# Longest-first order of the attention value products, two-queue load of the first block of x, and a replanned start, in a fused LayerNorm, window-attention and MLP kernel

## The chip, the cores and the metric

The kernel runs on one core of one Trainium2 chip. Times are microseconds (us) of device time for one execution. A profile's span is the part of it that the engines' records cover, here about 2 us less. A profile shows one execution.

Engine names: PE is TensorE's matmul, PEld its weight load, DVE is VectorE, ACT ScalarE, POOL GpSimd, SP SyncE.

## The reference

S = 2048 tokens, D = 512, bfloat16 in and out. A is causal attention over a window of 256 tokens, with 32 heads of 16; B is a gated MLP without an activation, with F = 1792.

```python
xn  = layernorm(x)                                   # no weights, eps 1e-5
qkv = (xn @ wqkv)                                    # 32 heads x 16
p   = softmax(where(0 <= i - j < 256, q @ k.T / 4, -1e9))
A   = (p @ v).reshape(S, D) @ wo
B   = ((xn @ w_gate) * (xn @ w_up)) @ w_down
out = x + A + B
```

## The kernel before

The kernel has a small planner: a list scheduler, run when the kernel is built, which emits the instructions of all engines in the order in which its own cost numbers say that they become ready. So a changed cost number changes the order of the program.

Work goes by chunks of 512 tokens (T = 0..3) and four groups of heads (c), which gives 16 **value blocks**. Keys and queries are in blocks of 64. A **segment** (k, q, m, at) says that key block k meets m query blocks from q on, and lies at block `at` of a strip P of exponentiated scores. Its m, times 64, is the number of columns of its matmuls.

```python
def layout(T):
    if T == 0:
        return [[(2, 2, 4, 0), (4, 4, 4, 4)], [(0, 0, 5, 0), (5, 5, 3, 5)],
                [(1, 1, 5, 0), (6, 6, 2, 5), (7, 7, 1, 7)], [(3, 3, 5, 0), (2, 6, 1, 5)]]
    return [[(3, 3, 5, 0), (-3, 0, 2, 5), (-4, 0, 1, 7)], [(2, 2, 5, 0), (6, 6, 2, 5), (7, 7, 1, 7)],
            [(0, 0, 5, 0), (5, 5, 3, 5)], [(1, 1, 5, 0), (-2, 0, 3, 5)], [(-1, 0, 4, 0), (4, 4, 4, 4)]]

def i_values(self, T, c, strips, banks):
    segments = [(P, s) for P, batch in strips for s in batch]
    for n, (P, (k, q, m, at)) in enumerate(segments):
        U, j = divmod(8 * T + k, 8)
        for lane in range(2):
            rows = slice(64 * lane, 64 * lane + 64)
            for e in range(4):
                self.nc.tensor.matmul(
                    banks[lane][32 * e:32 * e + 17, 64 * q:64 * (q + m)],
                    lhsT=self.V[U % 3][rows, j, 4 * c + e, 0:17],
                    rhs=P[rows, e, 64 * at:64 * (at + m)],
                    start=n == 0, stop=n == len(segments) - 1, tile_position=(64 * lane, 32 * e), ...)
```

One segment is a **round** of eight small matmuls, one on each 64 x 32 tile of the array, each with its own weight load just before it. I call load and matmul a **pair**. The first four blocks (T = 0) have 9 rounds, with lengths 4,4,5,3,5,2,1,5,1 in units of 64 columns (72 pairs). The other twelve have 12 rounds, 5,2,1,5,2,1,5,3,5,3,4,4 (96 pairs). All of a block's segments add into the same two banks, so their order is free.

The start, the weights of the planner and the loads:

```python
PACE = 2.95                       # the planner's distance between score batches, us
load(nc.sync, self.x[:, 0, :], xv[:, 0, :])
load(nc.scalar, self.x[:, 1, :], xv[:, 1, :])
for n, lo in enumerate((1024, 512, 0)):              # value, key, query weights
    load(nc.sync, self.Wqkv[:, :, lo:lo + 512], w["qkv"][:, :, lo:lo + 512])
    if n:
        load(nc.sync, self.x[:, n + 1, :], xv[:, n + 1, :])
# ... Wg, Wu, the rest of x, Wd in five pieces, Wo
o = self.pe(at, 1.25 if T else 0.87, f"V{v}")        # do_values: what the planner takes a value block to cost
land = (3.75, 3.9, 7.9, 9.6)                         # first_chunk: when blocks 0..3 of x are taken to land
wv, wk, wq = 6.1, 7.3, 9.1                           # and the three parts of Wqkv
```

In the first chunk the planner emits for each block of 128 tokens a *turn* (four transposing matmuls), values, keys and queries.

The softmax here doesn't subtract the row's maximum and nothing guards it: scores larger than these inputs give would overflow.

## Time and profile before

| | before |
|---|---|
| time, median of 3 runs | 267.49 us (267.42 to 268.14) |
| span of the profiled run | 266.0 us |
| PE busy | 97% of the span |
| value blocks: first matmul to the next dense one | 0.95 to 0.97 us (first four), 1.35 us (ten of the other twelve; 1.32 and 1.27 in the two at 203 and 247 us) |
| first gate matmul (the end of the start) | 18.06 us |

These lines are from the page of the kernel before. The first ones are the span and each engine's busy time, then the granted clock in 40 slices (9 is 90% or more) and the shares of the chain of work that ended last, by engine.

```profile
span 266.0 us, 7966 instructions
PE 257.9 (97%) x3423; PEld 131.4 (49%) x3458; DVE 192.8 (72%) x369; ACT 163.0 (61%) x118; POOL 119.8 (45%) x272
PEclk9999999999999999999999999999999999999999
PE 93%; DMA 3%; issue 1%; SPq 1%; DVE 1%
```

PE bounds the kernel. Only PE work that takes less time, an earlier start or a shorter tail can help. The waits view of PE (line: us in total, times, longest) names the few waits there are. All but the slivers called "issue" lie in the first 10 us:

```profile
PE M L203 <- issue: 1.3, 8, 0.2
PE M L193 <- PEq L790: 0.8, 1, 0.8
PE M L602 <- DVE xn L263: 0.4, 1, 0.4
PE M L663 <- ACT xnT L197: 0.3, 1, 0.3
PE M L203 <- DMA Wqkv<-in_A_wqkv_dram: 0.3, 1, 0.3
```

The timeline of PE at the start (start us, duration us, line, shape, count, and in brackets the idle time before it and what ended it), and one line of VectorE's: the first statistics, which start when block 0 of x has landed.

```profile
5.72 0.40 PE L602 MATMUL M<-ident,xn 128*128 128x128 bf16 x4 [0.41 <-DVE xn L263]
6.80 1.06 PE L663 MATMUL M<-Wqkv,xnT 128*64 128x256 bf16 x16 [0.34 <-ACT xnT L197]
9.38 2.85 PE L203 MATMUL M<-xnT,Wqkv 128*128 128x128 bf16 x48 [0.29 <-DMA Wqkv<-in_A_wqkv_dram]
12.07 0.39 PE L602 MATMUL M<-ident,xn 128*128 128x128 bf16 x4
18.06 1.03 PE L203 MATMUL M<-xnT,Wg 128*128 128x512 bf16 x3
3.78 0.69 DVE L576 BATCH_NORM_STATS2 st<-x 128x6 f32<-128x512 bf16 x1 [1.84 <-DMA x<-in_A_x_dram]
```

Turn 0 is at 5.72, the queries at 9.38 wait 0.29 us for their weights, turn 2 is at 12.07, and from the first gate matmul at 18.06 on PE hardly waits.

Two value blocks in the timeline of PE, one of 72 and one of 96 matmuls. The length of a block is the distance from its start to the start of the dense matmul on the next line.

```profile
35.42 1.04 PE L235 MATMUL M<-P,V 64*17 64x256 bf16 x72
36.39 0.39 PE L203 MATMUL M<-xnT,Wg 128*128 128x512 bf16 x1
...
100.30 1.42 PE L235 MATMUL M<-P,V 64*17 64x320 bf16 x96
101.65 1.04 PE L203 MATMUL M<-xnT,Wg 128*128 128x512 bf16 x3
```

The second block again in the windows view of the value line: stretch, then PE's and PEld's busy us with the number of instructions that run in the stretch (one can count in two), granted clock, DMA share, GB/s.

```profile
100.30:100.63 0.33, 0.33 (x32) 0.31 (x33) 1.00 0.07 25
100.63:100.95 0.32, 0.32 (x48) 0.31 (x29) 1.00 0.22 80
100.95:101.30 0.35, 0.35 (x40) 0.35 (x38) 1.00 0.90 290
101.30:101.65 0.35, 0.35 (x32) 0.13 (x14) 1.00 0.05 12
```

### The profile page before, as it was taken

To read this page: it belongs to the slowest core of one execution; us is meant where nothing else is said; L and a number is where in the kernel's file an instruction comes from. 1 tells how busy PE (TensorE), PEld (TensorE's weight loads), DVE (VectorE), ACT (ScalarE), POOL (GpSimd) and SP (SyncE) were. 2 spreads that over 40 slices of the span, in tenths; PEclk is the share of its full clock that TensorE was granted. 3 is DMA by queue.
4 is the path that set the end of the run, shared out by engine and by line. 5 is a ranking of instruction groups with operands and counts; after the bars stand their busy time and mean duration, and the time that the engine had idled before them with its cause. 6 is when DMAs were issued, how large, how long until landed. Compare 5 with 4: busy or idle time off the path is not lost.

```text
span 266.0 us, 7966 instructions
## 1 busy us (share of the span) xinstructions
PE 257.9 (97%) x3423; PEld 131.4 (49%) x3458; DVE 192.8 (72%) x369; ACT 163.0 (61%) x118; POOL 119.8 (45%) x272
## 2 busy tenths in 40 slices
PE   7999999999999999999999999999999999999995
PEld 7884444554445444465445354446544454444562
DVE  4889887888997628696997539787784439697504
ACT  3637676667667657678676566667876666656000
POOL 1403665654356361808265552708173543618000
PEclk9999999999999999999999999999999999999999
DMA  7999920000000400000002310000000000000002
GB/s 218 377 373 349 189 43 0 4 2 0 4 2 20 101 20 26 0 2 2 2 0 43 81 39 2 2 4 0 2 2 22 20 22 23 0 2 0 2 2 80
DMA packets 17251, 13.88 MB, mean 52 GB/s; under 512 B 7104, under 2 KB 17216, under 8 KB 17216
## 3 DMA queue, kind: packets, MB, share of 16 engines
q1 hardware_dynamic: 16928, 13.18, 16.9%
q8 instruction: 27, 0.44, 0.8%
q10 hardware_dynamic: 288, 0.20, 0.3%
q14 instruction: 8, 0.07, 0.1%
HBM read 9.70 MB, written 2.10 MB: 44 GB/s over the span
## 4 chain that ended last, share of the span: by engine, by line
PE 93%; DMA 3%; issue 1%; SPq 1%; DVE 1%
PE M L203 70%; PE S L211 9%; PE M L235 7%; PE M L663 5%; DMA Wqkv<-in_A_wqkv_dram 2%; SPq L148 1%; DMA out_dram<-xn 1%; PE S L203 1%; DVE xn L756 1%; PE M L602 0%
## 5 line engine op out<-in xcount | busy, mean ns | idle before, releaser
L487 ACT ACTIVATE P<-S 128x2048 bf16<-128x2048 f32 x76 | 140.9, 1853 | 61.0 <-PE S L211 54.2
L220 POOL TENSOR_SCALAR_AFFINE_SELECT P<-P 64x256 bf16<-64x256 bf16 (+1 forms) x248 | 112.8, 456 | 119.1 <-ACT P L487 106.3
L203 PE MATMUL M<-xnT,Wg 128*128 128x512 bf16 x216 | 57.1, 380 | 0.4
L203 PE MATMUL M<-xnT,Wu 128*128 128x512 bf16 x214 | 56.8, 380 | 0.5
L203 PE MATMUL M<-Wd,hT 128*128 128x512 bf16 (+1 forms) x215 | 50.4, 373 | 1.0 <-issue 0.8
L714 DVE TENSOR_TENSOR hT<-M,gsb 128x512 bf16<-128x512 f32 x56 | 38.0, 678 | 6.0 <-PE M L203 5.7
L199 DVE CAST gsb<-M 128x512 bf16<-128x512 f32 x43 | 29.4, 684 | 5.8 <-PE M L203 5.7
L203 PEld LDWEIGHTS <-hT 128*128 128x128 bf16 x238 | 21.6, 98 | 24.1 <-issue 3.1
L203 PEld LDWEIGHTS <-Wu 128*128 128x128 bf16 x224 | 20.5, 98 | 25.6 <-issue 2.9
L203 PEld LDWEIGHTS <-Wg 128*128 128x128 bf16 x224 | 20.0, 98 | 24.6 <-issue 3.3
L203 PE MATMUL M<-xnT,Wqkv 128*128 128x128 bf16 (+1 forms) x219 | 30.3, 286 | 0.7 <-DMA Wqkv<-in_A_wqkv_dram 0.3
L211 PE MATMUL S<-Q,K 32*128 32x320 bf16 (+3 forms) x720 | 30.1, 254 | 0.3
L523 DVE STREAM_TRANSPOSE at<-M 128x512 f32<-128x512 f32 x32 | 22.3, 707 | 9.2 <-PE M L235 9.1
L211 PEld LDWEIGHTS <-K 32*128 32x128 bf16 x720 | 11.9, 92 | 32.2 <-issue 31.3
L226 DVE TENSOR_TENSOR P<-P,masks 128x512 int16<-128x512 int16 x56 | 22.8, 412 | 6.4 <-ACT P L487 6.3
L274 DVE TENSOR_SCALAR K<-M,own 128x512 bf16<-128x512 f32 x28 | 20.1, 743 | 4.3 <-PE M L203 3.6
L756 DVE TENSOR_TENSOR y<-M,x 128x512 bf16<-128x512 f32 x12 | 8.2, 685 | 20.1 <-PE M L203 20.1
L203 PEld LDWEIGHTS <-Wqkv 128*128 128x128 bf16 x224 | 15.8, 98 | 11.5 <-issue 1.9
L235 PE MATMUL M<-P,V 64*17 64x320 bf16 (+4 forms) x1440 | 21.0, 252 | 0.0
L235 PEld LDWEIGHTS <-V 64*17 64x17 bf16 x1440 | 16.7, 85 | 2.3 <-issue 0.8
L663 PE MATMUL M<-Wqkv,xnT 128*64 128x256 bf16 x256 | 15.7, 274 | 0.3 <-ACT xnT L197 0.3
L203 PE MATMUL M<-Wo,OT 128*128 128x512 bf16 (+1 forms) x61 | 15.0, 372 | 0.4 <-issue 0.3
(51 smaller groups left out, 134.1 us busy)
## 6 DMA issues: line engine op xcount, KB each, us to landing
Wg<-in_B_w_gate_dram SPq DMA_DIRECT2D x2, 896.0 KB, 10.2
Wu<-in_B_w_up_dram SPq DMA_DIRECT2D x2, 896.0 KB, 12.2
Wqkv<-in_A_wqkv_dram SPq DMA_DIRECT2D x3, 512.0 KB, 5.7
Wd<-in_B_w_down_dram SPq DMA_DIRECT2D x4, 384.0 KB, 9.6
out_dram<-y SPq DMA_DIRECT2D x12, 128.0 KB, 1.7
x<-in_A_x_dram SPq DMA_DIRECT2D x1, 1024.0 KB, 14.2
x<-in_A_x_dram SPq DMA_DIRECT2D x1, 512.0 KB, 11.5
Wo<-in_A_wo_dram SPq DMA_DIRECT2D x1, 512.0 KB, 8.0
```

Of the source, the lines that this page charges most:

```text
L199: self.nc.vector.tensor_copy(out=out, in_=in_)
L203: self.nc.tensor.matmul(ps, lhsT=a, rhs=b, start=first and n == 0, stop=last and n == len(pairs) - 1)
L211: self.nc.tensor.matmul(self.S[:, e, 64 * at:64 * (at + m)], lhsT=self.K[U % 3][rows, c, j].rearrange("p l t -> p (l t)"), rhs=self.Q[T % ...
L220: self.nc.gpsimd.affine_select(out=v, in_=v, pattern=[[0, 4], [0, n], [sign, 64]], base=0, fill=0.0, compare_op=ALU.is_gt if kind else ALU ...
L226: self.nc.vector.tensor_tensor(out=v, in0=v, in1=m, op=ALU.bitwise_and)
L235: self.nc.tensor.matmul(banks[lane][32 * e:32 * e + 17, 64 * q:64 * (q + m)], lhsT=self.V[U % 3][rows, j, 4 * c + e, 0:17], rhs=P[rows, e, ...
L274: self.nc.vector.tensor_scalar(out=out, in0=in_, scalar1=own, scalar2=None, op0=ALU.mult)
L487: ex = self.op(f"exp{g}", {"A": (took + 0.06, took + 0.18)}, [o], lambda e: self.nc.scalar.activation(out=P[:, :, 0:hi], in_=self.S[:, :, ...
L523: t = self.op(f"tr{v}", {"V": (0.63, 0.71)}, [o] + ts, lambda e, par=par: nc.vector.transpose(out=self.at[:, :, par, :], in_=self.M[banks[ ...
L663: self.nc.tensor.matmul(self.M[i][64 * lane:64 * lane + 64, 256 * jj:256 * jj + 256], lhsT=self.xnT[T % 2][:, k, tok], rhs=w[:, lane], sta ...
L714: x = self.op(f"u{T}.{f}", {"V": PSUM_COPY["V"]}, [o, ("gate", T, f)], lambda e: self.nc.vector.tensor_tensor(out=self.hT[T % 2][:, f, :], ...
L756: self.nc.vector.tensor_tensor(out=keep["y"][:, cols], in0=self.M[i][:, cols], in1=self.x[:, t, cols], op=ALU.add)
```

## The change

The intent: put the long value products first so that the short ones come with their weights already loaded; get block 0 of x earlier by loading its halves on two queues; and tell the planner of the shorter value blocks and of the landing times, so that it emits the keys of blocks 0 and 1 ahead of their queries.

```diff
-    PACE = 2.95
+    PACE = 2.9
-        load(nc.sync, self.x[:, 0, :], xv[:, 0, :])
+        load(nc.sync, self.x[0:64, 0, :], xv[0:64, 0, :])
+        load(nc.scalar, self.x[64:128, 0, :], xv[64:128, 0, :])
-        for f, g in ((0, 3), (3, 6), (6, 9), (9, 12), (12, 14)):
+        for f, g in ((0, 4), (4, 8), (8, 11), (11, 14)):
             load(nc.sync, self.Wd[:, f:g], w["d"][:, f:g])
-        segments = [(P, s) for P, batch in strips for s in batch]
+        segments = sorted(((P, s) for P, batch in strips for s in batch), key=lambda x: -x[1][2])
-        o = self.pe(at, 1.25 if T else 0.87, f"V{v}")
+        o = self.pe(at, 1.12 if T else 0.80, f"V{v}")
-        land = (3.75, 3.9, 7.9, 9.6)
-        wv, wk, wq = 6.1, 7.3, 9.1
+        land = (3.75, 3.9, 7.9, 9.8)
+        wv, wk, wq = 6.1, 7.4, 9.4
```

The lengths become 5,5,5,4,4,3,2,1,1 and 5,5,5,5,4,4,3,3,2,2,1,1.

## The prediction

> **What bounds it now.** The page's busy table has PE at 97% of a 266.0 us span (VectorE 72%, ScalarE 61%, GpSimd 45%), the granted clock is full in every slice, and the chain of waits is 93% PE. The waits view gives PE under 4 us of waiting in all: 0.3 us for the query weights at 9.38 us, some at the start, the rest slivers of 0.2 us. Between dense 512-column matmuls the trace's starts lie 0.216 us apart practically everywhere, so there are no hidden stalls to win. Only two things can help: PE work that takes less time, or a PE that starts earlier. The tail (0.7 us of VectorE, 1.6 us of output DMA) is unchanged, and the last block's attention chain has about 7 us of slack before the output projection, so getting scores out earlier (pace 2.95 to 2.90) is worth about nothing.
>
> **Value products.** 16 blocks; timeline: first value matmul to the next dense one is 0.97 us for the first four (72 matmuls), 1.35 us for the other twelve (96). A round is 8 small matmuls on 8 tiles of the array. By their starts, a round that follows on takes 137, 110, 82, 56 or 28 ns for 320, 256, 192, 128 or 64 columns while instructions are queued ahead; once the queue has run dry, each matmul comes 8.4 ns after the last (67 ns a round). In the old order (5,2,1,5,2,1,...) early short rounds drain the queue: one block shows its second 128/64 pair taking 110 to 180 ns instead of 84. And it ends on a 256-column round: from its last start to the next dense matmul 0.20 us, after 64 columns 0.12. Longest first gives the queue time to stay full (17 ns consumed per matmul against 8.4 issued) and ends on 64 columns. [...] Sum of rounds 1.10 us plus the 0.12 us exit: 1.22 instead of 1.35, so 0.13 x 12; the first four already end on 64 columns and win about 0.02 each. Together 1.6 us, all on the critical path. The sort needs the last strip about 0.4 us earlier; GpSimd's last mask now finishes 1.1 us or more before it is read, so no new wait.
>
> **Head.** The build order becomes turn 0, values 0, turn 1, keys 0, keys 1, queries 0, queries 1. Keys 1 fill the wait for the query weights (last landing 9.33 us). The halves of x on two queues put block 0 at the front of both; I expect it 0.2 to 0.4 us earlier (first statistics now at 3.78), with block 1 later but within its slack. Turn 2 then comes at about 11.6 instead of 12.07, the first gate matmul at 17.5 instead of 18.06. Gain 0.5 us (0.2 to 0.8).
>
> **Costs.** [...] one value block now stands between dense matmuls instead of after scores: +0.1 us. Fewer, larger Wd loads: nothing.
>
> **Total.** 267.5 - 1.6 - 0.5 + 0.1 = 265.5 us, range 264.6 to 266.4. Faster by over 2%: 0.01; within 2%: 0.98; slower: 0.01.
>
> **Right if** value blocks of 96 measure 1.20 to 1.24 us and of 72 about 0.95, the query-weight wait is gone from the waits of PE, and the first gate matmul is near 17.5. **Wrong if** short rounds at the end still starve (blocks stay near 1.3), turn 3 waits for its normalised block so that the head gains nothing, a last strip comes late, or the replanned order brings stalls between dense matmuls.

The "queue" is the picture of loads that run ahead of their matmuls (33 loads in the first 0.33 us of a block); no record shows a queue itself. The 0.1 us was the estimate; in the trace before, the one value block that follows dense matmuls starts 309 ns after the start of the last of them, where most dense matmuls follow each other by 216 ns, so 0.09 us later.

## The result, and the profile after

| | before | after |
|---|---|---|
| time, median of 5 runs on the same chip | 268.05 us (267.42 to 268.24) | 268.04 us (267.54 to 268.15) |
| ratio after / before | | 1.0002, 95% interval 0.9985 to 1.0020 |

All ratios in this document are the mean time of one kernel's runs over that of the other's of the same rounds, so not quite the ratio of the medians. Executions over 1.5% slower than the fastest of the same kernel are left out of the means. All outputs are right. The change did nothing to the time. The range that was predicted, 264.6 to 266.4, does not hold 268.04.

The page after has the same picture (its fastest run was the one profiled: 267.54 us, the others had spans of 266.0 to 266.2). Its PE count is higher only because this trace has all 3458 matmul records and the one before lacks 35.

```profile
span 265.6 us, 7999 instructions
PE 260.2 (98%) x3458; PEld 131.9 (50%) x3458; DVE 189.5 (71%) x365; ACT 165.5 (62%) x122; POOL 119.8 (45%) x272
```

The start did in this trace what was foretold. The waits view of PE has no wait for Wqkv any more, and the timeline has turn 2 at 11.42 instead of 12.07 and the first gate at 17.41 instead of 18.06:

```profile
PE M L194 <- PEq L791: 0.8, 1, 0.8
PE M L603 <- DVE xn L264: 0.7, 1, 0.7
PE M L664 <- ACT xnT L198: 0.3, 1, 0.3
```

```profile
5.32 0.40 PE L603 MATMUL M<-ident,xn 128*128 128x128 bf16 x4 [0.67 <-DVE xn L264]
11.42 0.39 PE L603 MATMUL M<-ident,xn 128*128 128x128 bf16 x4
17.41 1.03 PE L204 MATMUL M<-xnT,Wg 128*128 128x512 bf16 x4
3.38 0.69 DVE L577 BATCH_NORM_STATS2 st<-x 128x6 f32<-128x512 bf16 x1 [1.44 <-DMA x<-in_A_x_dram]
```

The value blocks did not. In the timeline of PE, the block of 72 takes 35.82 - 34.77 = 1.05 us, longer than before (0.97), and the block of 96 takes 99.95 - 98.65 = 1.30 us (before 1.35, expected 1.22):

```profile
34.77 1.11 PE L236 MATMUL M<-P,V 64*17 64x320 bf16 x72
35.82 0.60 PE L204 MATMUL M<-xnT,Wg 128*128 128x512 bf16 x2
...
98.65 1.37 PE L236 MATMUL M<-P,V 64*17 64x320 bf16 x96
99.95 0.60 PE L204 MATMUL M<-Wo,OT 128*128 128x512 bf16 x2
```

To compare traces I cut each into three parts by the starts of two PE instructions, which any timeline of PE shows: the **start** (to the first gate matmul), the **chain** (from there to the last matmul's start) and the **tail** (from there to the end of the span). The last two columns are block lengths: the mean of the four blocks of 72, and the median of those blocks of 96 whose next matmul has a record.

| trace | start | chain | tail | block of 72 | block of 96 |
|---|---|---|---|---|---|
| before | 18.06 | 244.36 | 3.54 | 0.962 | 1.349 |
| after | 17.41 | 244.40 | 3.81 | 1.047 | 1.303 |

So the chain, on which the value blocks lie, has not become shorter at all; the start is 0.65 us shorter in this pair of traces; the tail is 0.27 us longer.

### The profile page after: what moved, and what is told of

Same layout as the page of the kernel before. It is cut to its first block, busy times and chain, and to the rows that moved or that the text cites. A ratio compares the mean times of both kernels' runs of the same rounds, so it can differ in the third digit from the quotient of the medians.

```text
span 265.6 us, 7999 instructions
## 1 busy us (share of the span) xinstructions
PE 260.2 (98%) x3458; PEld 131.9 (50%) x3458; DVE 189.5 (71%) x365; ACT 165.5 (62%) x122; POOL 119.8 (45%) x272
## 4 chain that ended last, share of the span: by engine, by line
PE 95%; DMA 2%; DVE 1%; ACT 0%; issue 0%; DVEq 0%
PE M L204 72%; PE S L212 9%; PE M L236 7%; PE M L664 6%; DMA x<-in_A_x_dram 1%; DMA out_dram<-xn 1%; PE S L204 1%; DVE xn L757 1%; PE M L603 0%; DVE st L577 0%; ACT xnT L198 0%; DVE xn L264 0%; ACT ve L581 0%; DVE mv L578 0%; DVE rs L584 0%
## 5 line engine op out<-in xcount | busy, mean ns | idle before, releaser
L204 PE MATMUL M<-xnT,Wg 128*128 128x512 bf16 x224 | 57.7, 380 | 0.0
L204 PE MATMUL M<-xnT,Wu 128*128 128x512 bf16 x224 | 57.7, 380 | 0.0
L204 PE MATMUL M<-Wd,hT 128*128 128x512 bf16 (+1 forms) x224 | 52.1, 373 | 0.0
L200 DVE CAST gsb<-M 128x512 bf16<-128x512 f32 x40 | 27.5, 686 | 5.3 <-PE M L204 5.0
L524 DVE STREAM_TRANSPOSE at<-M 128x512 f32<-128x512 f32 x32 | 21.4, 699 | 12.5 <-PE M L236 12.5
L236 PEld LDWEIGHTS <-V 64*17 64x17 bf16 x1440 | 17.7, 86 | 3.5 <-issue 1.3
L204 PE MATMUL M<-Wo,OT 128*128 128x512 bf16 (+1 forms) x64 | 16.2, 374 | 0.0
```

The source lines that it names most:

```text
L200: self.nc.vector.tensor_copy(out=out, in_=in_)
L204: self.nc.tensor.matmul(ps, lhsT=a, rhs=b, start=first and n == 0, stop=last and n == len(pairs) - 1)
L236: self.nc.tensor.matmul(banks[lane][32 * e:32 * e + 17, 64 * q:64 * (q + m)], lhsT=self.V[U % 3][rows, j, 4 * c + e, 0:17], rhs=P[rows, e, ...
L524: t = self.op(f"tr{v}", {"V": (0.63, 0.71)}, [o] + ts, lambda e, par=par: nc.vector.transpose(out=self.at[:, :, par, :], in_=self.M[banks[ ...
```

## The experiments

The first batch took the change apart and tried the theory that had formed, beside a control: the kernel before with one comment added.

**Theory A, a window of pairs in flight.** I read the load and matmul records of single blocks. In this table, from the trace before, block at 100.30, times are ns after the block's first matmul. "Place" is the number of the pair.

```
place  0   load at   -2   matmul at    0 (its record ends at 302)
place 31   load at  222
place 32   load at  227
place 33   load at  333   = 302 + 31
place 34   load at  341
place 35   load at  350
```

The loads of places 0 to 32 run ahead of their matmuls. The 34th waits until the first matmul has *ended*, although that matmul started 333 ns before, and after it loads come one per 8.3 ns. So A says: about 33 pairs are in flight, and the load at place p starts no earlier than 31 ns after the end of matmul p-33; loads that were held so follow at 8.3 ns. In addition, 32 places behind a matmul that raises a semaphore (in this block places 7, 11, 15, 31, 43, 47, 55, 91 and 95, where something is released for others), about 26 ns are lost: delays of 24 to 26 ns stand at places 39, 43 and 47, which are 7, 11 and 15 plus 32. The ends in the records are modelled by the profiler (its page's legend says so), so A is a rule fitted to records, not an observed mechanism. But it holds widely: in none of the 13 traces does a load from place 33 on start earlier than 30 ns after the end of the matmul 33 places before it. (Before place 33 another limit shows: no load starts before the matmul eight places earlier, the last one on its tile, has started; place 16 loads at 143, and matmul 8 starts at 141. The first eight matmuls of this block, one on each tile, start 3.3 ns apart, and on one tile a round follows one of 64 columns after 28 ns where nothing holds it.)

Counted in single instructions, there are 64 from matmul 0 to load 32 (32 matmuls and 32 loads), and matmul 32, the next one, starts in no block of the 13 traces earlier than 26 ns after the end of matmul 0. So the records fit a place that stays taken until its matmul ends; that is an inference from these starts and ends.

**Rival B** is the thought behind the change and the prediction: an entry is free when its matmul starts, so long rounds fill the queue and only early short rounds drain it. The load at 333 ns already speaks against it. **Rival C**: the sort needs the last strip of P earlier, and the blocks wait for its masks. In the trace after, blocks of 96 took 1.30 us whether the last mask was done 0.7 or 2.6 us before its strip was read, so C fell by the traces alone.

From A I worked out, with the lengths and semaphores of this kernel, what the 16 blocks take in sum: 19.80 us in the old order, 19.77 sorted. And I searched for an order that makes it small, the **planned order**: lengths 1,1,2,5,5,5,5,3,4,3,4,2 and 5,1,4,3,5,4,1,5,2, sum 18.36. Its idea: the first 33 pairs stand in the queue when the block begins (in the block above the loads of places 0 to 15 come 3.3 ns apart, not 8.3), so short rounds are cheap there; long rounds then let the window move on; no run of short rounds stands at the end.

### e1_control

```diff
+    # unchanged: the control
```

> The kernel before with one comment added, as a control: the ratio should be 1.000 and its interval shows what differences five rounds can resolve. If single runs scatter over 267.4 to 268.2 us here too, the scatter is not the change's; I expect that. Value blocks as before: about 0.96 us (72 matmuls) and 1.35 us (96).

Measured: 267.94 us (267.29 to 268.01), ratio 0.9998 [0.9986, 1.0011]. Its trace has the first gate at 17.59, where the kernel before had 18.06 and the same program. It does not wait for the query weights at all. So moments at the start differ by half a microsecond between executions of one program.

### e1_sort_only

```diff
-        segments = [(P, s) for P, batch in strips for s in batch]
+        segments = sorted(((P, s) for P, batch in strips for s in batch), key=lambda x: -x[1][2])
```

> The kernel before with only the value products sorted, longest first; nothing else moves. Theory of the prediction (a queue that stays full behind long rounds): blocks of 96 take 1.22 us and of 72 0.95, total 1.6 us less than the control. Rival, formed from the trace after (only about 33 load-and-matmul pairs are in flight; the next pair enters 31 ns after the matmul 33 places earlier has ended, then one pair per 8.3 ns; 26 ns more where the matmul 32 places earlier raised a semaphore): 1.30 us and 1.05 us, sum of the 16 blocks 19.8 us against 19.8 before, total within 0.1 us of the control.

Measured: 267.67 us (267.47 to 267.89), ratio 0.9993 [0.998, 1.0007]. The two blocks in the timeline of PE are 1.05 and 1.30 us long, as in the whole change:

```profile
35.68 1.11 PE L235 MATMUL M<-P,V 64*17 64x320 bf16 x72
36.73 0.39 PE L203 MATMUL M<-xnT,Wg 128*128 128x512 bf16 x1
...
100.86 1.37 PE L235 MATMUL M<-P,V 64*17 64x320 bf16 x96
102.16 0.39 PE L203 MATMUL M<-xnT,Wg 128*128 128x512 bf16 x1
```

The chain is 244.24, so 0.12 us shorter than the control's 244.36. The block lengths give the same: ten blocks of 96 win 0.047 us each, the one of 1.32 us wins 0.02, the one of 1.27 us loses 0.03, and the four of 72 lose 0.085 each. Where the sorted block loses is in its records (the whole change, block at 98.65, ns as above):

```
round (columns)  first load  first matmul     to the next round's first matmul
48..55 (192)        660          767           83
56..63 (192)        769          850           82
64..71 (128)        852          932           56
72..79 (128)        934          988           56
80..87 (64)        1017         1044           75   (28 if nothing held it)
88..95 (64)        1099         1119         last matmul at 1177
single loads: place 81 at 1041 (matmul 48 ended 1010), place 89 at 1123 (matmul 56 ended 1093)
```

The loads of the two last, shortest rounds wait for the *ends* of the 192-column rounds, 33 places before them. Long rounds first cannot help that: a window of 33 pairs that is full cannot get fuller. In the block's second half the short rounds use up the lead in time and end at the pace of the loads.

### e1_head_only

```diff
-        load(nc.sync, self.x[:, 0, :], xv[:, 0, :])
+        load(nc.sync, self.x[0:64, 0, :], xv[0:64, 0, :])
+        load(nc.scalar, self.x[64:128, 0, :], xv[64:128, 0, :])
-        for f, g in ((0, 3), (3, 6), (6, 9), (9, 12), (12, 14)):
+        for f, g in ((0, 4), (4, 8), (8, 11), (11, 14)):
-        land = (3.75, 3.9, 7.9, 9.6)
-        wv, wk, wq = 6.1, 7.3, 9.1
+        land = (3.75, 3.9, 7.9, 9.8)
+        wv, wk, wq = 6.1, 7.4, 9.4
```

> The kernel before with only the start of the change: first block of x in halves on two queues, the planner's landing times, fewer Wd loads; value order, value cost and pace as before. Theory: the first gate matmul starts near 17.4 us instead of 18.06 and, as PE has no other wait, the total falls by 0.6 us. Rival: the start's gain is taken back later or is within what single runs scatter, and the total stays within 0.2 us of the control.

Measured: 267.6 us (267.42 to 267.96), ratio 0.9993 [0.9981, 1.0006]. The start takes 17.97 us in this trace, so the 0.65 us of the first pair of traces is not repeated. In the waits view of PE there are two waits for weights, although block 0 landed as early (statistics at 3.38):

```profile
PE M L664 <- DMA Wqkv<-in_A_wqkv_dram: 0.4, 1, 0.4
PE M L204 <- DMA Wqkv<-in_A_wqkv_dram: 0.3, 1, 0.3
```

The second is that of the queries, at 10.18, although keys now stand before them. In the timeline of PE the first is the value product of block 0:

```profile
6.47 1.06 PE L664 MATMUL M<-Wqkv,xnT 128*64 128x256 bf16 x16 [0.40 <-DMA Wqkv<-in_A_wqkv_dram]
```

The kernel before started it at 6.80, after 0.34 us of waiting for ScalarE. So block 0 comes earlier (by 0.24 us in the mean of all traces, see below), but here what it needs next, the value weights, has not landed.

### e1_planned_order

One line is added to the kernel before; the list has the lengths given above.

```diff
         segments = [(P, s) for P, batch in strips for s in batch]
+        segments = [segments[i] for i in ((2, 5, 4, 0, 6, 8, 3, 7, 10, 9, 11, 1) if T else (2, 6, 1, 3, 4, 0, 8, 7, 5))]
```

> The kernel before with another order of the value segments alone, chosen by the in-flight rule: blocks of the first four chunks go 5,1,4,3,5,4,1,5,2 and the others 1,1,2,5,5,5,5,3,4,3,4,2 (columns in units of 64). In-flight theory: every block of 72 takes 0.94 us and every block of 96 1.22 us, the 16 blocks 18.4 us instead of 19.8, total 1.4 us less than the control. Rival (the order matters only through what the last round is, and through the queue being full early): short rounds at the front should hurt, blocks of 96 at 1.35 us or more, no gain.

Measured: 265.92 us (265.75 to 266.13), ratio 0.9928 [0.9916, 0.9941]. The chain is 242.89, shorter than the control's by 1.47; rule A gives 1.44. (Of the rest of the 2.0 us between the medians, 0.29 is a shorter tail in the trace, and what is left lies within the scatter of the start.) In the timeline of PE the blocks take 0.95 and 1.22 us:

```profile
35.22 1.02 PE L236 MATMUL M<-P,V 64*17 64x320 bf16 x72
36.17 0.39 PE L203 MATMUL M<-xnT,Wg 128*128 128x512 bf16 x1
...
99.92 1.29 PE L236 MATMUL M<-P,V 64*17 64x64 bf16 x96
101.14 1.04 PE L203 MATMUL M<-xnT,Wg 128*128 128x512 bf16 x3
```

The 1.22 us is the length that the prediction had promised for the sorted order. In this block the rounds after the first ones of 64, 64 and 128 columns start 35, 29 and 56 ns later, as if nothing held them, because all of these lie within the first 33 pairs.

### e2_short_first

```diff
-        segments = [(P, s) for P, batch in strips for s in batch]
+        segments = sorted(((P, s) for P, batch in strips for s in batch), key=lambda x: x[1][2])
```

> The kernel before with the value segments sorted the other way, shortest first; one look, for the length of the blocks alone. In-flight rule (about 33 pairs in flight, entry 31 ns after the matmul 33 places earlier ended, one pair per 8.3 ns, 26 ns more behind a signalling matmul): blocks of 72 take 0.99 us and blocks of 96 1.29 us, although the last round has 320 columns. Rival (what counts is that no short rounds come last, and the planned order won by that alone): short first should then be as good as the planned order but for a longer exit of about 0.08 us, 1.30 for 96 but 1.03 for 72, and the short rounds in front should take 56 and 28 ns like anywhere else with a full queue; the rule says the first long rounds come after them with a pause, because pair 33 must wait for the first matmul's end.

One look, so one run of unknown state: 267.05 us. The chain is 244.06, so 0.30 us shorter than the control's; rule A gives 0.31, and B would have this order, with its short rounds earliest, worse than the old one. The blocks take 1.00 and 1.30 us. The opposite of the change is a little better than the change. The rival named in the expectation, that only short rounds at the end matter, gave 1.30 us for the block of 96 too, so this length does not tell it from A; but it gave 1.03 for the block of 72, which took 1.00, and no pause at place 33, whose load comes at 227 ns, 31 ns after the end of the first matmul (block at 100.4).

### e3_late_signals

The lengths stay 5,2,1,5,2,1,5,3,5,3,4,4. Segments of equal length change places so that fewer early matmuls are the last to read something: the semaphores are raised at places 31, 55, 91 and 95 instead of nine places.

```diff
+        segments = [segments[i] for i in ((3, 1, 5, 0, 4, 2, 6, 7, 8, 9, 10, 11) if T else (0, 1, 2, 3, 4, 5, 6, 7, 8))]
```

> The kernel before; in the blocks of 96 the segments are swapped only against others of the same length, so that the row of lengths stays 5,2,1,5,2,1,5,3,5,3,4,4, but the matmuls that raise a semaphore for another engine move from places 7, 11, 15, 31, 43, 47, 55 to 31 and 55 (and the last two, as before). In-flight rule with 26 ns behind a signal: 1.27 us a block instead of 1.35, about 0.9 us in total, ratio 0.9965. Rival (only lengths matter, a signal costs nothing): blocks stay at 1.35 us and the total does not move.

Measured: 267.04 us (266.66 to 267.65), ratio 0.997 [0.9956, 0.9984]. The chain is 243.55, 0.81 us shorter than the control's; rule A gives 0.83. The block of 96 in the timeline of PE takes 1.27 us where it took 1.35, with the same lengths in the same order:

```profile
100.64 1.34 PE L236 MATMUL M<-P,V 64*17 64x320 bf16 x96
101.91 0.82 PE L203 MATMUL M<-xnT,Wg 128*128 128x512 bf16 x3
```

No thought of lengths alone explains this. The last matmul starts at 1070 ns into the block instead of 1147: three early signals, 26 ns each. The cost shows in the pairs 32 places further on, in the middle of a block (the 24 to 26 ns at places 39, 43 and 47 of the trace before). The kernel before has in its last block only the two final signals, and there too the last matmul starts at 1070 ns.

So far, the change of the chain against the control (us). The 16 measured block lengths, summed, change by the same -0.12, -0.30, -0.81 and -1.47 (where the record of the matmul after a block is missing, I took off the 226 ns to the one after it):

| order | rule A, sum of 16 blocks | measured chain |
|---|---|---|
| sorted, longest first | -0.03 | -0.12 |
| shortest first | -0.31 | -0.30 |
| old lengths, late signals | -0.83 | -0.81 |
| planned | -1.44 | -1.47 |

### e2_pace_only

```diff
-    PACE = 2.95
+    PACE = 2.9
-        o = self.pe(at, 1.25 if T else 0.87, f"V{v}")
+        o = self.pe(at, 1.12 if T else 0.80, f"V{v}")
```

> The kernel before with only the planner's numbers changed: pace 2.90 instead of 2.95 and value blocks counted at 1.12 and 0.80 us. Theory: PE stays dense, the number of mode changes is the same, so the total stays within 0.2 us of before. Rival: a tighter pace costs stalls between dense matmuls or moves value blocks away from scores (0.1 us each) and loses up to 0.5 us, which would be where the start's gain went.

Measured: 268.41 us (267.91 to 268.68), ratio 1.0015 [0.9995, 1.0034], so a loss that is not quite told from nothing. (A mode change in the expectation is a weight load of another tile shape than the one before it; the records have 177 in the trace before and 178 in the trace after, which has these numbers too.) The chain is 244.51, 0.15 us longer than the control's. In all 13 traces, value blocks that follow directly on dense matmuls are two where these numbers are changed and one where they are not; the chain is longer by 0.10 to 0.16 us in each of the three pairs that differ in these numbers (0.15 here, 0.16 from sort only to the whole change, 0.10 between the next two kernels). The records split it further. In this run three more blocks raise fewer early signals, so the 16 blocks are 0.09 us shorter, but one score batch, at 217.43, starts 0.15 us late; in the whole change one block, at 113.8, ends 0.07 us late. Without these, 0.09 to 0.10 us are left in each of the three pairs. I take the second value block after dense matmuls for the cause of that, but no run isolates it from the rest of the replanning.

### e2_planned_and_head, e2_planned_after

The first is the planned order with all of e1_head_only; the second is the whole change with the planned order in place of the sort, so it has the pace and cost numbers too.

```diff
 # e2_planned_and_head, against e1_head_only
         segments = [(P, s) for P, batch in strips for s in batch]
+        segments = [segments[i] for i in ((2, 5, 4, 0, 6, 8, 3, 7, 10, 9, 11, 1) if T else (2, 6, 1, 3, 4, 0, 8, 7, 5))]
 # e2_planned_after, against the changed kernel
-        segments = sorted(((P, s) for P, batch in strips for s in batch), key=lambda x: -x[1][2])
+        segments = [(P, s) for P, batch in strips for s in batch]
+        segments = [segments[i] for i in ((2, 5, 4, 0, 6, 8, 3, 7, 10, 9, 11, 1) if T else (2, 6, 1, 3, 4, 0, 8, 7, 5))]
```

> The planned order of the value segments and the start of the change together, pace and planner costs as before. Blocks 0.95 and 1.22 us. If the two parts add up: 1.9 us (planned order, measured) and 0.2 us (start, measured, not clear of zero) less than before, so about 265.7 us and ratio 0.992. If the start were worth the 0.5 us of the prediction, 265.3.

Measured: 265.87 us (265.41 to 266.03), ratio 0.9916 [0.9895, 0.9937]: the planned order alone gave 0.9928, so nothing is added that can be told apart.

> The changed kernel with its sort replaced by the planned order, all else of the change kept (pace 2.90, planner costs, start). Blocks 0.95 and 1.22 us; 1.4 to 1.9 us less than before, ratio 0.993 to 0.995. If the pace does harm it should be slower than the planned order with the start alone, by more than 0.3 us.

Measured: 266.93 us (266.39 to 267.18), ratio 0.9957 [0.9938, 0.9976]. That is 1.06 us slower than planned_and_head. By the traces, 0.10 of it is the chain, 0.49 the tail (3.80 against 3.31) and 0.34 the start. Both kernels have the same loads, so the 0.34 is scatter of the start between executions. This execution shows what the halves of x on two queues can push back. These are VectorE's statistics of blocks 0 and 1 and PE's first value product and turn 1 in the timeline:

```profile
3.33 0.69 DVE L578 BATCH_NORM_STATS2 st<-x 128x6 f32<-128x512 bf16 x1 [1.39 <-DMA x<-in_A_x_dram]
6.53 0.69 DVE L578 BATCH_NORM_STATS2 st<-x 128x6 f32<-128x512 bf16 x1 [1.31 <-DMA x<-in_A_x_dram]
6.80 1.06 PE L665 MATMUL M<-Wqkv,xnT 128*64 128x256 bf16 x16 [0.70 <-DMA Wqkv<-in_A_wqkv_dram]
8.47 0.40 PE L604 MATMUL M<-ident,xn 128*128 128x128 bf16 x4 [0.60 <-DVE xn L265]
```

Block 0 is there at 3.33, but the value weights only at 6.80, and block 1 at 6.53, so turn 1 waits until 8.47 (7.80 in the kernel before). Over all traces the first statistics start at 3.63 us on average with one load (eight traces, 3.45 to 3.78) and at 3.39 with two halves (five, 3.33 to 3.48), and in three of these five traces, but in none of the eight, the first value product then waits 0.4 to 0.7 us for its weights.

### e3_after_five_wd

The tail is 3.8 us in both kernels that have all the numbers of the change, and 3.25 to 3.6 in the others. A theory: four larger pieces of Wd instead of five smaller leave the queue in a different state. The whole change, with the five pieces back:

```diff
-        for f, g in ((0, 4), (4, 8), (8, 11), (11, 14)):
+        for f, g in ((0, 3), (3, 6), (6, 9), (9, 12), (12, 14)):
```

> The changed kernel with the Wd loads in five pieces again. In the traces of the two kernels that have all of the change's planner numbers, 3.8 us pass between the start of the last matmul and the end, in the others 3.25 to 3.6, and the difference lies in the queue's closing instructions, after the last data have landed. If that comes of how many instructions stand in that queue, the tail returns to 3.3 to 3.6 us and the total falls by about 0.3 us; rival: the tail stays at 3.8 and the total is the changed kernel's, 268.0.

Measured: 268.02 us (267.68 to 268.14), ratio 1.0002 [0.999, 1.0014], tail 3.78. The theory falls. In the traces before and after, the last output data land 2.40 and 2.41 us after the last matmul's start, and the difference of the tail lies in what the engines do after that to close the program. Why it differs between programs stays open.

### e3_planned_keys_first

The best of the parts: the planned order, and of the change only the landing numbers, which give the new order of keys and queries. One load of block 0, five pieces of Wd, old pace.

```diff
+        segments = [segments[i] for i in ((2, 5, 4, 0, 6, 8, 3, 7, 10, 9, 11, 1) if T else (2, 6, 1, 3, 4, 0, 8, 7, 5))]
-        land = (3.75, 3.9, 7.9, 9.6)
-        wv, wk, wq = 6.1, 7.3, 9.1
+        land = (3.75, 3.9, 7.9, 9.8)
+        wv, wk, wq = 6.1, 7.4, 9.4
```

> The planned value order with only the landing times of the change (keys of two blocks, then queries), without the halves of x. If the halves bring nothing (block 1 of x and the weights land later for it), this equals the planned order with the whole new start, 265.9 us, ratio 0.992; if the halves bring 0.3 us, it is 266.2.

Measured: 265.47 us (265.25 to 265.85), ratio 0.9912 [0.9898, 0.9925] against the kernel before (267.82 in this batch). It is the fastest of all kernels here by its median and beats both, though planned_and_head (0.9916 in another batch) is not told from it. The span from its page is 263.8 us. Its whole waits view of PE has no weights in it:

```profile
PE M L193 <- PEq L791: 0.8, 1, 0.8
PE M L664 <- ACT xnT L197: 0.3, 1, 0.3
```

And two lines of its timeline of PE:

```profile
7.92 3.85 PE L203 MATMUL M<-xnT,Wqkv 128*128 128x128 bf16 x64
17.60 1.03 PE L203 MATMUL M<-xnT,Wg 128*128 128x512 bf16 x4
```

From 7.92 on, 64 key and query matmuls run without a wait for weights: that the keys of block 1 stand where the query weights used to be awaited works. But with the planned order alone (0.9928 in another batch) the interval overlaps, so the gain of the keys-first order by itself is not told from nothing.

All traces together (us; each is one execution):

| trace | start | chain | tail | block of 72 | block of 96 |
|---|---|---|---|---|---|
| before | 18.06 | 244.36 | 3.54 | 0.962 | 1.349 |
| control | 17.59 | 244.36 | 3.54 | 0.962 | 1.350 |
| sort only | 18.32 | 244.24 | 3.32 | 1.047 | 1.303 |
| head only | 17.97 | 244.34 | 3.59 | 0.960 | 1.348 |
| pace only | 18.71 | 244.51 | 3.58 | 0.961 | 1.348 |
| short first | 18.02 | 244.06 | 3.27 | 1.002 | 1.301 |
| late signals | 18.46 | 243.55 | 3.28 | 0.962 | 1.272 |
| planned order | 17.86 | 242.89 | 3.25 | 0.948 | 1.222 |
| planned and head | 17.93 | 242.88 | 3.31 | 0.948 | 1.222 |
| planned, keys first | 17.60 | 242.89 | 3.27 | 0.949 | 1.223 |
| after | 17.41 | 244.40 | 3.81 | 1.047 | 1.303 |
| after, five pieces of Wd | 17.92 | 244.40 | 3.78 | 1.048 | 1.303 |
| planned in after | 18.27 | 242.98 | 3.80 | 0.949 | 1.222 |

The chain repeats to 0.02 us between kernels that share order and numbers; the start does not. So an effect of a tenth of a microsecond can be read in the chain from one trace, but not in the total.

## Why the prediction was wrong

- **What bounds it: right.** PE is at 97 to 98%, and every gain that was measured came from PE taking less time.
- **Value products: wrong, and this is the step that failed.** The prediction said: "Longest first gives the queue time to stay full (17 ns consumed per matmul against 8.4 issued) and ends on 64 columns." Both numbers are right, and so are the round times and the exit of about 0.12 us after a 64-column round (0.119 to 0.122 us from the start of its last matmul in the blocks of 72 before). What is wrong is that the queue can get ahead without end. By the records, about 33 pairs are in flight, and a place is free only when a matmul ends, 190 to 300 ns after its start. So the short rounds at the end are issued at 8.3 ns a pair again, or wait for ends. The term was 1.6 us; the blocks in sum, and so the chain, gave 0.12. The size of 0.13 us for a block of 96 became 0.047, and the blocks of 72, which should have won 0.02, lost 0.085. The prediction named this itself under "Wrong if": short rounds at the end still starve. The numbers to refuse it were in the trace at hand: 33 loads and no 34th in the first 0.33 us of a block. It also laid the slow second 128/64 pair to drainage by lengths alone, where three semaphores a block cost 26 ns each.
- **Start: the mechanism is half right, the size is not secured.** The first statistics came 0.24 us earlier, inside 0.2 to 0.4, and turn 2 and the first gate stood in the trace after where they were foretold (11.42 and 17.41). That they stood there is in part luck: the control, with the old start, has the first gate at 17.59. And "block 1 later but within its slack" fails in one trace (turn 1 at 8.47), and the 0.5 us was sized from a single trace, with a wait for query weights that the same program does not always have: over seven traces with the old start the first gate is at 17.59 to 18.71, mean 18.15; over five with the whole new start at 17.41 to 18.27, mean 17.90. The mean gain is 0.25 us, and the timed runs (0.9993, interval 0.9981 to 1.0006) do not tell it from none.
- **Costs: about right.** +0.1 us was expected for the value block between dense matmuls; the three pairs of chains give 0.10 to 0.16, of which 0.09 to 0.10 can belong to it, and the kernel with these numbers alone was not faster (1.0015). Fewer, larger pieces of Wd are worth nothing, as expected (1.0002 on both sides of that experiment).
- **Tail: "unchanged" was wrong.** It is 0.27 us longer in the trace. It is not the pieces of Wd; its cause is open.

The sum with measured terms is: chain +0.04 (sort -0.12, planner's numbers +0.16), start -0.25, tail +0.27, together +0.06 us. Measured: -0.01 us between the medians.

## What to carry to other kernels

By rule A, which fits the records of this kernel, a stream of small matmuls on separate tiles was limited by how many pairs are in flight until their *end*; where a trace shows the same (a load that waits for the end of the matmul 33 places back, here 333 ns into the block against 302 ns for that end), put short ones where the queue has been filled beforehand (the start of the block), long ones after them while it refills, and do not end on a run of short ones: the planned order, made so, took 1.22 us for a block of 96, where the old order took 1.35 and the sorted one 1.30. A matmul that raised a semaphore cost the pairs 32 places behind it 24 to 26 ns here, so let the last reader of a buffer come late in a block; that alone gave 0.8 us in the chain with no other change. Size a gain at the start from several traces of the same program, and run a change's planner numbers as a part of their own, since they can give back what another part won.
